# One tiling for value and background matmuls: 128-wide matmuls written as four column tiles

## The chip, the cores and the metric

The kernel runs on one core of one Trainium2 chip. The metric is the device time of one execution in microseconds; the median of three runs stands for a kernel. Durations and waits come from one profiled execution. In its rows PE is the matmul engine (TensorE), PEld its weight loads, DVE, ACT and POOL are the vector, activation and general engines, SP issues DMAs.

## The reference

A transformer block over 2048 rows of 640 values in bfloat16: layer norm, attention with 32 heads of 20, a residual, a second layer norm, a gated feed-forward of 1728 with a second residual.

```python
def _A_ref(x, wqkv, wo):
    ...
    scores = jnp.einsum("bhqd,bhkd->bhqk", q, k) * (Dh ** -0.5)
    p = _softmax(scores, axis=-1)
    o = jnp.einsum("bhqk,bhkd->bhqd", p, v)
    ...
h = x + _A_ref(_layernorm(x, axis=-1), A_wqkv, A_wo)
# _B_ref: h_ = gelu(x @ w_gate) * (x @ w_up); return h_ @ w_down
h2 = h + _B_ref(_layernorm(h, axis=-1), B_w_gate, B_w_up, B_w_down)
```

## The kernel before

**Chunks and slots.** The rows are cut into seven query chunks of 512, 512, 256, 256, 256, 128 and 128 rows, numbered 0 to 6. The heads form eight groups of four; a slot is one group at 512 rows, two at 256, four at 128. A slot goes through all 2048 keys in units of two or three score tiles of 512 columns, held in the PSUM banks 0 to 2 and 3 to 4 in turn.

**Three kinds of matmul.** A score matmul (line 919, helper `qk_mms`) has 32 rows of weights, the tile position (32 j, 0) for head j of the group, and so a row tile of the array. A value matmul (`pv_op`, recorded at line 359 with `v_all` among its inputs) uses all 128 rows and 21 columns of weights, 20 values and a column of ones for the sum, at the tile position (0, 32 j): four heads sit beside each other as four column tiles and write four strips of 32 partitions of bank 6. All others use the whole 128 x 128 array: projections of q, k, v and of the attention output (`chain`, line 640; wo is the latter's weight), gate and up (`mms`, line 1095), down (line 1159), transposes (lines 585 and 1002), bounds of the scores (`q_bound`, line 732, 32 columns of weights, and `q_bound0`, line 752), and warming matmuls that write nothing of use.

**Around them.** ACT takes exponentials of the score tiles; a part of the tiles goes to DVE instead (line 840 and the operations after it), which approximates the exponential by sums of four terms. After a slot, DVE copies bank 6 to `osb`, the sums go through small DMAs and a reciprocal, POOL scales, and DMAs put the rows into memory. `post` then does for one chunk: loading the attention rows, wo, residual (line 1063), layer norm, transposition (by DMA, for the last chunk on PE), gate, gelu (by tanh on ACT, or by its table for the last chunk), up and product (lines 1131, 1148, 1120), down, residual (line 1163) and the output DMA. It runs while the next chunk's scores are being made; these "background" operations use the banks that are left, 7 and 5.

**Who sets the order.** The program is listed as operations with their engine, estimated duration, priority, inputs and outputs. `Sched.schedule` plays them through a model of the engines and writes one fixed order per engine; `emit` adds the semaphores. Priorities go from scores (0) over value matmuls (1), slot ends (2) and layer norm (2.5) to background (3). Every PE operation has a mode, "row", "col" or "full". A change of mode costs 0.098 us in the model. Lines that use it:

```python
MODE_SWITCH = {"pe": .098, "act": 1.28}
...
if chosen is None:
    chosen, banks = o, got
    if e != "pe" or p[0] < 1 or o.mode == mode[e] or t - o.ready > PE_AGE:
        break
elif o.mode == mode[e]:
    chosen, banks = o, got
    break
```

So PE takes the ready operation of highest priority, but below the scores it prefers one of the present mode, unless the first has been ready for over 1.5 us (PE_AGE). An operation below the scores is not started if it, with its switch, would run past the time at which the next scores are due. Where PE would be idle for long, the model inserts warming matmuls.

## Time and profile before

| what | value |
|---|---|
| median of 3 runs | 899.54 us (898.82 to 899.83) |
| profiled execution: its own time, its span | 899.9 us, 898.2 us |
| PE busy | 836.4 us |
| ACT busy | 851.0 us |
| DVE busy | 689.6 us |
| matmuls of PE, weight loads | 10745, 10809 |
| mean granted clock of PE | 0.998 |

The span is the time from the first to the last instruction of the profiled execution; the rest of its own time lies around it. A busy PE is not a PE at its peak: matmuls are pipelined, a busy stretch includes their latency and short pauses between them. The start of one matmul less the start of the one before says more than the duration of either. A row such as "128\*21 128x256" names the weights (128 rows, 21 columns) and the streamed operand (128 partitions, 256 columns). Some matmul records are missing, so that the weight loads of a line count its matmuls better.

### The profile page before, as it was taken

How to read it: one execution, taken by the hardware profiler on the slowest of the kernel's cores; microseconds unless marked ns; L12 is line 12 of the kernel's file. 1: busy time of each engine (PE TensorE's matmuls, PEld its weight loads, DVE VectorE, ACT ScalarE, POOL GpSimd, SP SyncE). 2: the span in 40 equal slices, each digit the busy share in tenths (PEclk: the TensorE clock that was granted, in tenths of full speed). 3: DMA queues.
4: the chain of work that ended last, by engine and by line, in shares of the span. 5: the costliest groups of instructions: out<-in, count | busy, mean ns of one | idle time of the engine just before them, and what ended most of it. 6: DMA issues, size and time to landing. Idle time of an engine off the chain costs nothing.

```text
span 898.2 us, 24425 instructions
## 1 busy us (share of the span) xinstructions
PE 836.4 (93%) x10745; PEld 359.1 (40%) x10809; DVE 689.6 (77%) x1263; ACT 851.0 (95%) x777; POOL 75.0 (8%) x147
## 2 busy tenths in 40 slices
PE   3999999899989899999999899999999999999988
PEld 2532222222223222323344333334445446666657
DVE  7839888888989888787778889965669669658553
ACT  6699999999999999999999999999999999999960
POOL 5000000000001100000000100000102000020100
PEclk9999999999999999999999999999999999999999
DMA  7211120222244510000111110011111010031000
GB/s 264 84 50 49 32 67 29 64 81 66 73 137 135 152 46 17 17 14 5 39 51 54 33 34 17 18 30 48 29 54 33 18 48 18 20 63 26 10 17 15
DMA packets 55937, 46.17 MB, mean 51 GB/s; under 512 B 25492, under 2 KB 49392, under 8 KB 55832
## 3 DMA queue, kind: packets, MB, share of 16 engines
q1 hardware_dynamic: 55832, 44.62, 17.8%
q8 instruction: 84, 1.38, 0.6%
q14 instruction: 21, 0.17, 0.1%
HBM read 30.68 MB, written 11.04 MB: 46 GB/s over the span
## 4 chain that ended last, share of the span: by engine, by line
ACT 46%; PE 46%; DVE 6%; issue 1%; DMA 1%; DVEq 0%
ACT pts L359 35%; PE ps L919 14%; PE ps L359 11%; ACT rege L359 10%; PE ps L1095 9%; PE ps L640 6%; PE ps L1159 5%; DVE rege L359 1%; DVE qt_all L359 1%; DVE rege L840 1%; ACT qt_all L359 1%; DVE stats L359 1%; DVE rege L1131 1%; PE ps L585 1%; DMA rege<-xn_t 1%
## 5 line engine op out<-in xcount | busy, mean ns | idle before, releaser
L359 ACT ACTIVATE pts<-ps 128x1536 bf16<-128x1536 f32 x578 | 652.6, 1242 | 10.2 <-PE ps L919 5.7
L919 PE MATMUL ps<-qt_all,kt_all 32*128 32x256 bf16 (+2 forms) x3584 | 320.8, 288 | 25.7 <-ACT pts L359 16.7
L919 PEld LDWEIGHTS ps<-qt_all,kt_all 32*128 32x128 bf16 x3584 | 103.3, 92 | 236.0 <-ACT pts L359 128.3
L840 DVE TENSOR_SCALAR rege<-ps 128x512 int16<-128x512 f32 x200 | 137.0, 687 | 58.6 <-PE ps L919 56.4
L359 ACT ACTIVATE rege<-ps 128x1536 bf16<-128x1536 f32 x115 | 172.1, 1496 | 1.5 <-PE ps L359 0.7
L1095 PE MATMUL ps<-rege,regw 128*128 128x256 bf16 (+2 forms) x951 | 151.6, 289 | 8.4 <-DVE rege L359 2.9
L359 PE MATMUL ps<-pts,v_all 128*21 128x256 bf16 (+2 forms) x2472 | 134.0, 287 | 0.0
L359 PE MATMUL ps<-rege,v_all 128*21 128x512 bf16 (+2 forms) x1564 | 127.6, 312 | 1.3 <-DVE rege L359 1.0
L840 DVE TENSOR_SCALAR qt_all<-ps 128x512 int16<-128x512 f32 x116 | 79.8, 688 | 42.5 <-PE ps L919 40.9
L1095 PEld LDWEIGHTS ps<-rege,regw 128*128 128x128 bf16 x980 | 74.2, 99 | 65.7 <-issue 31.5
L359 POOL TENSOR_TENSOR on<-osb,bsum 128x512 bf16<-128x512 f32 x30 | 42.0, 1399 | 648.2 <-DMA bsum<-rsums 648.1
L359 DVE TENSOR_SCALAR rege<-rege 128x2048 int16<-128x2048 int16 x132 | 92.7, 717 | 2.1 <-PE ps L359 1.2
L640 PE MATMUL ps<-regw 128*128 128x512 bf16 (+1 forms) x340 | 82.0, 349 | 4.6 <-issue 1.7
L1159 PE MATMUL ps<-regw,rege 128*128 128x320 bf16 x448 | 83.7, 302 | 1.1 <-DVE rege L1120 0.5
L359 PEld LDWEIGHTS ps<-pts,v_all 128*21 128x21 bf16 x2472 | 54.3, 91 | 32.4 <-issue 24.4
L359 DVE TENSOR_SCALAR qt_all<-qt_all 128x2048 int16<-128x2048 int16 (+2 forms) x111 | 64.7, 594 | 2.0 <-PE ps L359 1.0
L359 PEld LDWEIGHTS ps<-rege,v_all 128*21 128x21 bf16 x1564 | 41.0, 90 | 45.9 <-issue 23.6
L359 PE MATMUL ps<-qt_all,v_all 128*21 128x256 bf16 (+2 forms) x1048 | 53.7, 282 | 1.7 <-DVE qt_all L359 1.6
L1159 PEld LDWEIGHTS ps<-regw,rege 128*128 128x128 bf16 x448 | 36.6, 97 | 35.8 <-issue 20.1
L359 DVE TENSOR_SCALAR qt_all<-rege 128x2048 int16<-128x2048 int16 x70 | 48.9, 707 | 0.9 <-PE ps L359 0.4
L640 PEld LDWEIGHTS ps<-regw 128*128 128x128 bf16 x360 | 28.9, 98 | 47.5 <-issue 25.0
L1148 DVE TENSOR_TENSOR rege<-rege,ps 128x512 bf16<-128x512 bf16 (+1 forms) x53 | 35.8, 677 | 15.6 <-PE ps L1095 15.4
(98 smaller groups left out, 503.2 us busy)
## 6 DMA issues: line engine op xcount, KB each, us to landing
bsum<-rsums SPq DMA_DIRECT2D x120, 64.0 KB, 2.0
rege<-in_A_x_dram SPq DMA_DIRECT2D x6, 640.0 KB, 5.1
q_rows<-regw SPq DMA_DIRECT2D x20, 128.0 KB, 1.9
out_dram<-rege SPq DMA_DIRECT2D x16, 160.0 KB, 2.2
attn<-on SPq DMA_DIRECT2D x120, 20.0 KB
regw<-in_B_w_gate_dram SPq DMA_DIRECT2D x5, 432.0 KB, 3.3
regw<-in_B_w_up_dram SPq DMA_DIRECT2D x5, 432.0 KB, 3.2
kt_all<-k_rows SPq DMA_DIRECT2D x12, 160.0 KB
```

Of the source, the lines that this page charges most:

```text
L359: return lambda eng: getattr(eng, method)(*args, **kwargs)
L585: op("pe", lambda eng, a=a: eng.transpose(bank16(bk, D)[:, 128 * a:128 * a + 128], src[:, a * 128:(a + 1) * 128], ident[:]), 0.055, prio, ...
L640: yield op("pe", lambda eng, l=l, r=r, k=k: eng.matmul(bank(bk, n), l, r, start=(k == 0), stop=(k == len(steps) - 1)), c_mm(n), prio, mode ...
L840: d_ops.append(op("dve", lambda eng: eng.tensor_scalar(v[:, 512 * h:512 * h + 512], bank(b), EXP_MUL, -32000.0, ALU.mult, ALU.max), c_dve( ...
L919: return lambda eng: eng.matmul(out()[:, kk * nq:(kk + 1) * nq], kt_all[32 * j:32 * j + 32, g, kt * 128:(kt + 1) * 128], qt_all[32 * j:32 ...
L1095: op("pe", lambda eng, a=a, f=f, fi=fi: eng.matmul(bank(bk)[:, fi * nq:(fi + 1) * nq], w[:, a, F0[f]:F0[f] + 128], hnT[:, a, 128 * tb:128 ...
L1131: op("dve", lambda eng, bg=bg, fv=fv, w=w: eng.tensor_scalar(fv, bank(bg, w), 0.5, None, ALU.mult), c_dve(w), p, reads=[kg], writes=hkeys( ...
L1148: hdone.append(op("dve", lambda eng, bu=bu, fv=fv, w=w: eng.tensor_tensor(fv, fv, bank(bu, w), ALU.mult), c_dve(w), p, reads=[ku] + hkeys( ...
L1159: op("pe", lambda eng, f=f, o=o, hf=hf, bk=bk: eng.matmul(bank(bk, 320), ha_f[:, o:o + 128], wd[:, f, hf * 320:(hf + 1) * 320], start=(f = ...
```

## The change

A new helper `col4` writes a matmul with 128 columns of weights as four with 32 columns each, at the tile positions (0, 0), (0, 32), (0, 64) and (0, 96), each into its strip of 32 partitions of the same bank, all with the same streamed operand. The four are one operation with the estimated duration of one. It is used in `chain` (all projections and wo), `mms` (gate and up), down and the warming matmuls. The matmuls of `q_bound` keep their number and get the tile position (0, 0). All these now have the mode "col", as value matmuls have. Transposes and `q_bound0` stay "full".

```diff
-                                o.fns, o.mode = [self.warm[b]], "full"
+                                o.fns, o.mode = self.warm[b], "col"
...
-                yield op("pe", lambda eng, l=l, r=r, k=k: eng.matmul(
-                    bank(bk, n), l, r, start=(k == 0), stop=(k == len(steps) - 1)),
-                    c_mm(n), prio, mode="full", util=n / 2400.0, reads=reads, writes=[key], acq=[bk] if (k == 0 and acq) else [],
+                yield op("pe", col4(lambda bk=bk: bank(bk, n), l, r, k == 0, k == len(steps) - 1),
+                    c_mm(n), prio, mode="col", util=n / 2400.0, reads=reads, writes=[key], acq=[bk] if (k == 0 and acq) else [],
                     after=after if k == 0 else ())
+
+        def col4(out, l, r, start, stop):
+            return [lambda eng, j=j: eng.matmul(out()[32 * j:32 * j + 32], l[:, 32 * j:32 * j + 32], r, start=start, stop=stop,
+                                                tile_position=(0, 32 * j), skip_group_check=True) for j in range(4)]
...
-                    bank(bk)[0:32, :], sel[:, t, :], aq[t], start=(k == 0), stop=(k == len(ts) - 1)),
-                    c_mm(512), prio, mode="full", util=0.05, reads=[aqk(t), ("sel", t)], writes=[key],
+                    bank(bk)[0:32, :], sel[:, t, :], aq[t], start=(k == 0), stop=(k == len(ts) - 1),
+                    tile_position=(0, 0), skip_group_check=True),
+                    c_mm(512), prio, mode="col", util=0.05, reads=[aqk(t), ("sel", t)], writes=[key],
...
-                        op("pe", lambda eng, a=a, f=f, fi=fi: eng.matmul(
-                            bank(bk)[:, fi * nq:(fi + 1) * nq], w[:, a, F0[f]:F0[f] + 128], hnT[:, a, 128 * tb:128 * tb + nq],
-                            start=(a == 0), stop=(a == NA - 1)),
-                           c_mm(nq), p, mode="full", util=nq / 2400.0, reads=hk + [(wkey, 0)], writes=[key], acq=[bk] if st else [],
+                        op("pe", col4(lambda fi=fi: bank(bk)[:, fi * nq:(fi + 1) * nq], w[:, a, F0[f]:F0[f] + 128],
+                                      hnT[:, a, 128 * tb:128 * tb + nq], a == 0, a == NA - 1),
+                           c_mm(nq), p, mode="col", util=nq / 2400.0, reads=hk + [(wkey, 0)], writes=[key], acq=[bk] if st else [],
...
-                        op("pe", lambda eng, f=f, o=o, hf=hf, bk=bk: eng.matmul(
-                            bank(bk, 320), ha_f[:, o:o + 128], wd[:, f, hf * 320:(hf + 1) * 320],
-                            start=(f == 0), stop=(f == NF - 1)), c_mm(320), p, mode="full", util=0.133, reads=hkeys(f // fn_) + [("wd", 0), "wd2", "wdz"],
+                        op("pe", col4(lambda bk=bk: bank(bk, 320), ha_f[:, o:o + 128], wd[:, f, hf * 320:(hf + 1) * 320],
+                                      f == 0, f == NF - 1), c_mm(320), p, mode="col", util=0.133, reads=hkeys(f // fn_) + [("wd", 0), "wd2", "wdz"],
...
-        sc.warm = {b: I("matmul", PS[:, 512 * b:512 * b + 512], kt_all[:, 0, 0:128], kt_all[:, 0, 0:512], start=True, stop=True,
-                        skip_group_check=True) for b in sc.warm_banks}
+        sc.warm = {b: col4(lambda b=b: PS[:, 512 * b:512 * b + 512], kt_all[:, 0, 0:128], kt_all[:, 0, 0:512], True, True)
+                   for b in sc.warm_banks}
```

## The prediction

> **What bounds the kernel now.** I read the page first: shares of engines, then the chain.

> ```profile
> span 898.2 us, 24425 instructions
> ...
> PE 836.4 (93%) x10745; PEld 359.1 (40%) x10809; DVE 689.6 (77%) x1263; ACT 851.0 (95%) x777; POOL 75.0 (8%) x147
> ...
> ACT 46%; PE 46%; DVE 6%; issue 1%; DMA 1%; DVEq 0%
> ```

> ACT and PE are both near full and share the chain, so neither share says where a saving counts. The busy time by stretches does:

> ```profile
> 725.00:750.00 25.00, 25.00 (x394) 13.63 (x393) 18.21 (x32) 24.85 (x23) 1.28 (x1) 1.00 0.13 37
> 775.00:800.00 25.00, 25.00 (x654) 15.74 (x640) 16.84 (x34) 24.73 (x23) 4.57 (x15) 1.00 0.23 41
> 850.00:875.00 25.00, 20.55 (x377) 14.88 (x377) 12.47 (x33) 17.01 (x19) 0.00 (x0) 0.96 0.05 15
> 875.00:900.00 25.00, 19.84 (x260) 17.28 (x257) 7.49 (x14) 2.96 (x6) 0.00 (x0) 0.97 0.04 14
> ```

> Columns after the length: PE, PEld, DVE, ACT, POOL, granted clock, DMA. From 50 to 859 us ACT runs exponentials back to back (their last ends at 858.9, from ACT's timeline); there a faster PE cannot move ACT by more than the few waits it has. From 859 on ACT is nearly idle, and 39.3 us are left. PE's timeline shows what fills them:

> ```profile
> 858.22 2.35 PE L1159 MATMUL ps<-regw,rege 128*128 128x320 bf16 x16
> 860.41 0.33 PE L1095 MATMUL ps<-rege,regw 128*128 128x128 bf16 x3
> ...
> 873.54 0.93 PE L1095 MATMUL ps<-rege,regw 128*128 128x128 bf16 x7 [2.87 <-DVE rege L359]
> ...
> 874.80 6.57 PE L1095 MATMUL ps<-rege,regw 128*128 128x128 bf16 x101
> 881.20 3.97 PE L1159 MATMUL ps<-regw,rege 128*128 128x320 bf16 x28
> 885.01 5.86 PE L1095 MATMUL ps<-rege,regw 128*128 128x128 bf16 x102
> 891.38 3.98 PE L1159 MATMUL ps<-regw,rege 128*128 128x320 bf16 x28 [0.52 <-DVE rege L1120]
> ```

> A chunk of 128 rows has 70 gate, 70 up (L1095) and 28 down (L1159) matmuls. So the last 16 down matmuls of chunk 4 and the whole feed-forward of chunk 5 come after the last exponential, although chunk 5's attention ended at 801.5 (copy of its accumulator): background work is late. Of 101 + 102 after 874.80, 140 are chunk 6's own, 63 chunk 5's.

> **What the change removes.** Switches of PE's tiling. One stretch of PE's timeline has them all:

> ```profile
> 846.78 0.42 PE L919 MATMUL ps<-qt_all,kt_all 32*128 32x128 bf16 x12
> 847.13 0.63 PE L359 MATMUL ps<-pts,v_all 128*21 128x128 bf16 x32
> 847.69 0.45 PE L1159 MATMUL ps<-regw,rege 128*128 128x320 bf16 x2
> 848.07 0.40 PE L919 MATMUL ps<-qt_all,kt_all 32*128 32x128 bf16 x12
> ```

> Score matmuls (row tiles) start at 846.78, value matmuls (column tiles) at 847.13, full ones at 847.69, scores at 848.07. Eight steps of four value matmuls at 56 ns are 0.45 us, yet the next group starts 0.56 later: 0.11 for the switch. Two of 320 columns (0.136 each) take 0.27 of 0.38: 0.11 again. Over the timeline of PE, start of a group less start and streaming time of the last matmul before, the median is 91 to 101 ns for each of the six kinds. There are 1627 switches, about 160 us of PE; 223 are between column and full tiles and cost nothing afterwards: 223 x 0.098 = 21.9 us. Those from and to row tiles stay, as every score group stands between two others. By time: 60 before 270 us, 140 from 270 to 747, 22 to 859, 1 later. Before 270 there is no feed-forward to be late (chunk 0's starts at 308), so I count 162 x 0.098 = 15.9 us.

> **What it adds.** About 2019 full matmuls (counted by their weight loads: 980 L1095, 448 L1159, 520 L640, 71 warming) become 8076, with as many weight loads of 32 columns. The nearest row is the value matmul: four of them start 3 to 4 ns apart, and the next four follow after 56 ns (128 columns) or 109 (256); full steps have 56 and 109, and 216 at 512 in both inside a run. The four tiles stream beside each other, with new weights at every step. Hence zero per step is my value. The bounds: the first step of a value run is 7 to 8 ns longer (117 at 256), and each new step is an operation of its own with its own semaphore update, so +8 a step is possible; weight loads of 32 columns (L732, not tiled) take 93 against 90 to 91 of the value's 21, and four in series would add 12 more: 0 to 20 ns a step; nothing below, since streaming is no shorter. Issue: the densest 128 PE instructions of the trace take 1.0 us, the densest 256 take 2.8; the tail's steps of 128 columns need 256 in 1.8. If the queue were held to 2.8, a step would take 88 ns and the 203 late ones 6.5 us more; I take 0, as the 128 go at the needed rate, and keep 6.5 as the end.

> Transposes (L585, L1002) stay full, so their neighbours now switch: 11 times from 17 to 28 us, 6 in the tail. At the start at most 11 x 0.1 = 1.1 us, in part under PE's waits for ACT and DVE: 0.5. In the tail two of three groups lie on the path: 0.4. Score bounds (L732) change tiling only, at the same length. The written order is planned anew, with value and background matmuls in one class: no switch is charged between them, so background fits into more gaps, and value matmuls go first instead of waiting behind a run of full ones. ACT's excess over its steady pitch between 50 and 868 us is some 20 us in all, near 1 us per 50 outside the ends; I move it by nothing and keep 2 us each way.

> **Sum.** From 803 to 860 PE gets through chunk 4's feed-forward (140 x 0.109 + 56 x 0.136 = 22.9 us) and chunk 5's wo (1.4): 43% of the time. Its start at 802.9 waited for the transposed rows (DMA, 0.25), not for PE; but their wo began at 775.65, when the attention rows (issued 763.90, 3.4 us to landing) had been there for 8 us, while PE was full (25.00 of 25). The 13.7 us saved from 270 to 747 clear that queue, so I take those 8 us and no more: the data cap it. Saved from 747 to 859: 2.2 us, or 5 us of elapsed time at 43%. Chunk 4 then ends at 860.4 - 13 = 847.4, just after chunk 5's rows are there (transpose issued 842.2, 2.7 us). Until 858.9 PE does 11.5 x 0.43 = 4.9 us of chunk 5's 12 (140 x 0.056 + 28 x 0.136 = 11.6, and gaps). The 7.1 left fit between 859 and 874.8, where chunk 6's own path (transposes, wo, switches) needs 3.4 of 15.9 us and PE waits 4.5 us today. So 63 x 0.062 + 28 x 0.137 = 7.8 us go from the end. What is late next is chunk 6's own chain, wo, layer norm, gate, up, down. Back come 0.5, 0.4 and 0.2 for a longer half-clock stretch (13 steps of 107 ns at 875 now, after an idle PE). 898.2 - 7.8 + 1.1 = 891.5 of span; the profiled execution took 899.9, 1.7 more, so 893.2; it lies 0.4 above the median 899.54: **892.8 us**. If chunk 5's tanh no longer delays the square root (table load at 871.2, after tanh at 870.1), the norm comes 1 to 2 us sooner: own range 888 to 896.

> [...] The trace has value steps with four weight loads of 21 columns every 56 ns. [...]

> **Rivals.**
> 1. Forecast: backlog cleared, 0.55.
> 2. Weight loads bind the short steps, 0.08. If the value's 56 ns already were the limit of its 84 columns, 128 columns take 85: +29 on 140 steps of chunk 6 and some 60 others, 4 to 6 us, which eats most of the gain: 897 to 899, and up to 902 if twice that. Against it: 21 and 32 columns differ by 3 ns as rows. [...]
> 3. Nothing is gained, 0.12: chunk 4 and 5 are held by banks and DMA chains, not PE (start at 802.9 after a DMA), so the tail stays: 898 to 901.
> 4. Slower, 0.25: each four-tile step costs p more than the planner is told, on all 1600 background steps after 270. It gains 15.9 and loses 1600 p; from p = 10 ns the backlog grows, and all of it lands in the tail. At 15 ns: +8.1, 907.6; at 20: +16, 915.6. PE at 25.00 of 25 gives it no room; interior value steps at 56 and 109 speak against it.

> That the switches stay is excluded by the value groups: tiles of one tiling follow each other at 56 ns.

> Faster by over 0.2% (1.8 us, about what a measurement of this kernel can tell from no change): 0.55. Within: rival 3 and half of 2, 0.16. Slower: rival 4 and half of 2, 0.29. The range for 8 in 10: 887.5, below the forecast's own, to 908, which leaves out rival 4 beyond 15 ns.

> **What would show it.** Right: no 0.1 us between value and background groups; chunk 4's last down before 850; fewer than 70 L1095 of chunk 5 after 859; the last L1095 group after 874 with some 140 steps, not 203; last exponential at 859 within 2 us. Wrong: four-tile steps over 66 ns at 128 or 119 at 256 (rivals 2, 4); ACT waiting for L919 between 50 and 859; a tail of 39 us as now (rival 3).

## The result and the profile after

The changed kernel takes **921.43 us** (median of 4 runs, 920.31 to 926.06), the kernel before 899.68 beside it: ratio 1.0253, 95% interval 1.0221 to 1.0284. It is slower by 21.8 us, outside the predicted range. The profiled execution is the longest of its four (926.06), so its sums are some 4 us larger than the difference of the medians. A helper takes the lines on by about four: scores are L923 now, every four-tile matmul has the line of `col4`, L645.

The page of the changed kernel, the same lines as before:

```profile
span 924.3 us, 36732 instructions
...
PE 851.3 (92%) x16930; PEld 375.0 (41%) x16930; DVE 687.7 (74%) x1263; ACT 853.1 (92%) x777; POOL 73.3 (8%) x147
...
ACT 46%; PE 39%; DVE 8%; DMA 4%; issue 2%; POOL 1%; SPq 0%; DVEq 0%; POOLq 0%
```

PE's matmuls and weight loads have grown from 21,554 to 33,860, by what the prediction counted and 16 more warming operations (87, before 71). The busy times of ACT and DVE are within 2.1 us of those before, so for them the 26.1 us of span are idle time. I cut the span at the first and at the last exponential of the scores (ACT's timeline):

| | before | changed | difference |
|---|---|---|---|
| first exponential starts | 35.6 | 38.6 | +3.0 |
| first to last exponential | 823.3 | 839.4 | +16.1 |
| last exponential to the end ("tail") | 39.2 | 46.3 | +7.1 |

**The middle.** The 693 exponentials come in the same order in both kernels, so the delay of each against the kernel before can be read. It is 2.9 us at the first and 0.3 from the ninth on (48 us): the late start is made up. At the last it is 19.0.

ACT's waits for scores have grown (total, times, longest; before, the first row was 5.7, 7, 3.7):

```profile
ACT pts L359 <- PE ps L923: 20.7, 25, 5.3
ACT rege L359 <- PE ps L923: 5.2, 7, 1.5
```

Busy time by stretches says where. Here ACT (fourth engine) is below 22 of 25 us, and so is the granted clock (three columns from the end), which was 1.00 in all stretches of the kernel before up to 850:

```profile
75.00:100.00 25.00, 23.55 (x250) 6.53 (x249) 18.64 (x35) 21.04 (x20) 1.27 (x1) 0.80 0.12 32
125.00:150.00 25.00, 23.52 (x238) 6.12 (x240) 18.45 (x35) 20.79 (x19) 1.27 (x1) 0.73 0.21 53
275.00:300.00 25.00, 22.27 (x218) 5.61 (x216) 14.42 (x26) 16.57 (x14) 1.27 (x1) 0.66 0.49 152
```

The clock was at half for 10.2 us from 84.3, 13.7 from 135.5 and 17.1 from 282.3, 41.0 us in all. From the start of each of these stretches to 3 us behind its end the delay grows from 0.1 to 3.5, from 3.9 to 8.8 and from 9.5 to 17.9 us: 16.7 of the 19.0 us arise there. PE's timeline just ahead of the first of them:

```profile
79.98 0.39 PE L923 MATMUL ps<-qt_all,kt_all 32*128 32x512 bf16 x3
80.31 0.39 PE L735 MATMUL ps<-sq,sel 128*32 128x512 bf16 x1
81.33 1.61 PE L923 MATMUL ps<-qt_all,kt_all 32*128 32x512 bf16 x8 [0.63 <-ACT pts L359]
83.34 0.32 PE L645 MATMUL ps<-regw 128*32 128x320 bf16 x4 [0.41 <-DVE rege L844]
```

For three microseconds PE has little but scores, which wait for ACT to free their banks; no value or background group stands between them. PE looks busy, as a score matmul of 512 columns is recorded for 0.39 us, but little streams through it. Count each matmul by its columns / 2400 us, as the kernel's own `util` does (0.213 us for 512 columns, where the traces have 0.216 from step to step), and by a quarter of that if it is one of four tiles, row or column. Then PE streams some 0.2 of its time in the 3.4 us from 80.2; in the kernel before no 3.4 us between 50 and 860 us fall much below 0.3 (the lowest has 0.28, at 115.9).

**The tail.** PE's timeline at its end:

```profile
902.03 3.28 PE L645 MATMUL ps<-rege,regw 128*32 128x128 bf16 x203
907.09 1.97 PE L645 MATMUL ps<-rege,regw 128*32 128x128 bf16 x128 [1.78 <-issue]
911.11 1.97 PE L645 MATMUL ps<-rege,regw 128*32 128x128 bf16 x128 [2.05 <-issue]
914.86 1.61 PE L645 MATMUL ps<-rege,regw 128*32 128x128 bf16 x101 [1.77 <-issue]
917.07 4.41 PE L645 MATMUL ps<-regw,rege 128*32 128x320 bf16 x112 [0.60 <-DVE rege L1123]
```

128 matmuls with 128 weight loads are 256 instructions. They run at the full rate (32 steps in 1.8 us, 56 ns each) and then PE stands for 1.8 to 2.1 us with nothing to wait for that the profile shows ("issue"). The DMA rows name the limit: the queue of kind "instruction" that serves PE has 132 packets of 16 KB here (84 before), one for each 256 of its 33,860 recorded instructions (21,554 before), and never two within 3.3 us (smallest distance 3.35). From the last exponential on these pauses add up to 10.3 us.

### The profile page after: what moved, and what is told of

Same layout as the page of the kernel before. It is cut to its first block, busy times and chain, and to the rows that moved or that the text cites. A ratio compares the mean times of both kernels' runs of the same rounds, so it can differ in the third digit from the quotient of the medians.

```text
span 924.3 us, 36732 instructions
## 1 busy us (share of the span) xinstructions
PE 851.3 (92%) x16930; PEld 375.0 (41%) x16930; DVE 687.7 (74%) x1263; ACT 853.1 (92%) x777; POOL 73.3 (8%) x147
## 4 chain that ended last, share of the span: by engine, by line
ACT 46%; PE 39%; DVE 8%; DMA 4%; issue 2%; POOL 1%; SPq 0%; DVEq 0%; POOLq 0%
ACT pts L359 35%; PE ps L645 18%; PE ps L923 12%; ACT rege L359 9%; PE ps L359 9%; DVE rege L844 2%; DMA regw<-in_A_wqkv_dram 1%; DVE qt_all L359 1%; DVE qt_all L844 1%; ACT qt_all L359 1%; DMA rege<-xn_t 1%; DMA sums<-osb 1%; DVE rege L359 1%; PE ps L585 0%; DVE xn_t L359 0%
## 5 line engine op out<-in xcount | busy, mean ns | idle before, releaser
L359 ACT ACTIVATE pts<-ps 128x1536 bf16<-128x1536 f32 x578 | 656.0, 1258 | 22.0 <-PE ps L923 20.7
L923 PE MATMUL ps<-qt_all,kt_all 32*128 32x256 bf16 (+2 forms) x3584 | 324.1, 292 | 21.9 <-ACT pts L359 14.4
L923 PEld LDWEIGHTS ps<-qt_all,kt_all 32*128 32x128 bf16 x3584 | 101.2, 92 | 260.5 <-ACT pts L359 145.3
L645 PE MATMUL ps<-rege,regw 128*32 128x256 bf16 (+2 forms) x3920 | 166.0, 289 | 16.4 <-issue 10.3
L359 ACT ACTIVATE rege<-ps 128x1536 bf16<-128x1536 f32 x115 | 173.6, 1510 | 5.6 <-PE ps L923 5.2
L359 PE MATMUL ps<-pts,v_all 128*21 128x256 bf16 (+2 forms) x2472 | 136.7, 291 | 0.0
L359 PE MATMUL ps<-rege,v_all 128*21 128x512 bf16 (+2 forms) x1564 | 132.3, 321 | 1.5 <-DVE rege L359 1.2
L844 DVE TENSOR_SCALAR qt_all<-ps 128x512 int16<-128x512 f32 x116 | 79.7, 687 | 41.3 <-PE ps L923 39.6
L645 PEld LDWEIGHTS ps<-rege,regw 128*32 128x32 bf16 x3920 | 81.9, 96 | 61.7 <-issue 32.5
L645 PE MATMUL ps<-regw 128*32 128x512 bf16 (+1 forms) x1440 | 94.5, 360 | 4.7 <-DVE rege L844 2.4
L359 DVE TENSOR_SCALAR rege<-rege 128x2048 int16<-128x2048 int16 x132 | 88.8, 690 | 4.0 <-PE ps L359 3.4
L359 POOL TENSOR_TENSOR on<-osb,bsum 128x512 bf16<-128x512 f32 x30 | 38.8, 1293 | 639.0 <-DMA bsum<-rsums 639.0
L645 PE MATMUL ps<-regw,rege 128*32 128x320 bf16 x1792 | 82.3, 301 | 2.3 <-DVE rege L1151 1.2
L359 PEld LDWEIGHTS ps<-pts,v_all 128*21 128x21 bf16 x2472 | 53.1, 91 | 36.0 <-issue 30.8
L359 DVE TENSOR_SCALAR qt_all<-qt_all 128x2048 int16<-128x2048 int16 (+3 forms) x111 | 63.2, 583 | 1.9 <-PE ps L359 0.9
L359 PEld LDWEIGHTS ps<-rege,v_all 128*21 128x21 bf16 x1564 | 42.1, 91 | 41.2 <-issue 21.1
L359 PE MATMUL ps<-qt_all,v_all 128*21 128x256 bf16 (+2 forms) x1048 | 55.2, 284 | 1.6 <-DVE qt_all L359 1.1
L645 PEld LDWEIGHTS ps<-regw 128*32 128x32 bf16 x1440 | 34.8, 98 | 45.7 <-issue 19.1
L645 PEld LDWEIGHTS ps<-regw,rege 128*32 128x32 bf16 x1792 | 42.1, 96 | 25.0 <-issue 10.6
L359 DVE TENSOR_SCALAR qt_all<-rege 128x2048 int16<-128x2048 int16 x70 | 48.9, 709 | 0.9 <-PE ps L359 0.4
```

The source lines that it names most:

```text
L359: return lambda eng: getattr(eng, method)(*args, **kwargs)
L645: return [lambda eng, j=j: eng.matmul(out()[32 * j:32 * j + 32], l[:, 32 * j:32 * j + 32], r, start=start, stop=stop, tile_position=(0, 32 ...
L844: d_ops.append(op("dve", lambda eng: eng.tensor_scalar(v[:, 512 * h:512 * h + 512], bank(b), EXP_MUL, -32000.0, ALU.mult, ALU.max), c_dve( ...
L923: return lambda eng: eng.matmul(out()[:, kk * nq:(kk + 1) * nq], kt_all[32 * j:32 * j + 32, g, kt * 128:(kt + 1) * 128], qt_all[32 * j:32 ...
```

## The experiments

Theory A: the middle is lost by lulls in the new order, in which PE's granted clock falls to half; the tail by the fetch of PE's instructions; the start by the order. Theory B: four-tile matmuls count less than full ones for what halves the clock. Each expectation was on record before its run.

**Old order, new instructions.** Every `mode="col"` of the change is "full" again for the planner; what is written stays four tiles.

```diff
-                    c_mm(n), prio, mode="col", util=n / 2400.0, ...
+                    c_mm(n), prio, mode="full", util=n / 2400.0, ...
```

> Four-tile instructions as in the changed kernel, but the planner is told the old modes, so every engine has the order of the kernel before. Theory A (the half-clock stretches at 84, 135 and 282 us come from lulls in the new order; the tail from PE's instruction fetch): no half clock before 860, first exponential at 35.6 and last at 859 within 2 us, but the tail has pauses of 1 to 2 us after every 256 PE instructions and is 46 to 51 us long instead of 39: 906 to 912. Theory B (column tiles count less for the clock gate than full matmuls do): half-clock stretches between 75 and 300 us here too, last exponential 868 or later, 915 or more.

Measured: 907.71 us, 1.0086 (1.0058 to 1.0115). First exponential 36.7, last 856.2, no half clock before 870, tail 48.2 with pauses of 0.5 to 1.9 us. The same stretches of this kernel:

```profile
75.00:100.00 25.00, 23.06 (x309) 7.34 (x309) 21.03 (x37) 24.46 (x22) 1.27 (x1) 1.00 0.11 31
125.00:150.00 25.00, 23.18 (x312) 7.53 (x308) 20.57 (x36) 24.95 (x23) 1.27 (x1) 1.00 0.06 18
275.00:300.00 25.00, 22.73 (x316) 7.02 (x308) 23.48 (x49) 25.00 (x24) 6.02 (x15) 1.00 0.43 126
```

The clock is full and ACT too, with the four-tile instructions of the changed kernel. Theory B falls.

**New order, old instructions.** `col4` writes one full matmul.

> The order of the changed kernel, but with full 128 x 128 matmuls again, so that switches between value and background groups, which this order does not plan for, cost some 0.1 us each on PE. Theory A: half-clock stretches near 84, 135 and 282 us as in the changed kernel, first exponential 38.6, last 875 or later; no pauses at 256 instructions in the tail, which is 39 us or less: 908 to 925. Theory B: no half clock before 860, last exponential 861 to 868, 900 to 908.

Measured: 933.99 us (runs from 922.56 to 937.08, the longest of them profiled), 1.0333 (1.0262 to 1.0405). First exponential 38.7; half clock for 51.2 us, from 75.3, 246.0 and 293.7; last exponential 900.6; tail 34.7 without pauses. The order alone brings the late start and the half clock. The size was missed. Of the 41.7 us by which its last exponential is late, 19.9 arise in the half-clock stretches. Another 13.5 come after 315 us, at full clock; that fits the 327 switches between value and background groups that this order does not plan, about 0.1 us each in this trace, but was not tested by itself.

**Parts of the change.** First with the projections, bounds and warming matmuls full, then with the chunks of 128 rows full as well.

```diff
+        def one(out, l, r, start, stop):
+            return [lambda eng: eng.matmul(out(), l, r, start=start, stop=stop, skip_group_check=True)]
...
-                        op("pe", col4(lambda fi=fi: ...
+                        op("pe", (col4 if nq > 128 else one)(lambda fi=fi: ...
```

> Projections of q, k and v, bounds and warming matmuls full as before, in mode and instruction; wo, gate, up and down in four tiles. Theory A: first exponential at 35.6, and no half clock near 84 and 135 us, since the old order of chunk 0 is back; the one near 282 may stay (8 us) or go; the tail has the pauses and is 45 to 47 us: 903 to 913. Theory B: no half clock before 250 either (few four-tile matmuls there), but one after 300 us where feed-forward is all there is: 912 or more.

Measured: 913.17 us, 1.0144 (1.0117 to 1.0171). First exponential 36.2, one half-clock stretch of 3.4 us at 130, last 864.1, tail 48.1. The time lies 0.2 us above theory A's range and within theory B's, the tail 1 us above A's, and A had no half clock near 135 us; but what B asks for, half clock after 300 us, is not there.

> As the one with full projections, and besides it the chunks of 128 rows keep full matmuls for wo, gate, up and down. If the pauses in the tail are PE's instruction fetch, they go, the tail is 39 us or less and the time lies 6 to 10 us below that of the kernel with full projections alone: 893 to 901. If the pauses have another cause (short steps of any kind), the tail stays at 45 us or more and the time within 2 us of that kernel.

Measured: 903.25 us, 1.0047 (1.003 to 1.0064), 9.9 below the run before it; tail 39.1 without pauses. The tail is settled, but the time was expected at 893 to 901: the backlog should have shrunk, and did not.

**The fetch by itself.** The kernel before, with only gate and up of the chunks of 128 rows written in m tiles of 128 / m columns, planned as before. With m = 4 a step of 56 ns has 8 PE instructions, with m = 2 it has 4, so that 256 of them last 3.6 us.

```diff
+                        op("pe", [lambda eng, a=a, f=f, fi=fi, j=j: eng.matmul(
+                            bank(bk)[64 * j:64 * j + 64, fi * nq:(fi + 1) * nq], w[:, a, F0[f] + 64 * j:F0[f] + 64 * j + 64],
...
+                            tile_position=(0, 64 * j), skip_group_check=True) for j in range(2)] if nq == 128 else
```

> The kernel before, with only gate and up of the chunks of 128 rows as four tiles of 32 columns, planned as before: 8 PE instructions a step. Fetch theory: pauses of 1.2 to 2.2 us after each 256 instructions in the tail, which grows by 7 to 9 us to 46 to 48; exponentials end at 859 as before: 906 to 909.

Measured: 908.62 us, 1.0096 (1.0063 to 1.0129); last exponential 857.9, tail 47.2.

> The kernel before, with gate and up of the chunks of 128 rows as two tiles of 64 columns: 4 PE instructions a step instead of 2, and planned as before. If the limit is one fetch of 256 instructions per 3.4 to 3.7 us, 64 steps of 56 ns (3.6 us) just fit: pauses of 0.2 us or less at each block, tail 39 to 40.5 us, time 899 to 901. [...]

Measured: 901.1 us, 1.0014 (0.9999 to 1.0029); tail 39.0. PE's timeline, four tiles first:

```profile
887.66 3.75 PE L1095 MATMUL ps<-rege,regw 128*32 128x128 bf16 x255
893.32 1.97 PE L1095 MATMUL ps<-rege,regw 128*32 128x128 bf16 x127 [1.91 <-issue]
897.23 0.57 PE L1095 MATMUL ps<-rege,regw 128*32 128x128 bf16 x26 [1.94 <-issue]
```

and two tiles, the same 102 steps:

```profile
883.84 5.88 PE L1095 MATMUL ps<-rege,regw 128*64 128x128 bf16 x204
```

With two tiles there is not one pause, and the steps are those of full matmuls (102 in 5.86 us before). It is the count of instructions, not tiling as such: twice the instructions cost nothing, four times cost 8.2 us of tail (47.2 against 39.0; 39.2 in the kernel before).

**The half clock by itself.** Two runs: the changed kernel with more warming, and the kernel before with none.

```diff
-WARM_WIN, WARM_MIN = 3.4, 0.5
+WARM_WIN, WARM_MIN = 3.4, 0.65
```

> The changed kernel, with the planner's bound for warming raised from 0.5 to 0.65 of PE's time in 3.4 us, so that it fills lulls with more warming matmuls. Theory A (lulls in the new order bring the half clock, which holds up ACT by some 16 us): the half-clock stretches before 300 us go, exponentials end at 860 to 866, the tail keeps its pauses: 904 to 911. If the half clock is no consequence of lulls, it stays and the time is 918 or more.

Measured: 921.19 us, 1.0247 (1.0214 to 1.0279). The half clock went from 41.0 to 6.8 us before the last exponential and the middle from 839.4 to 829.9, as A has it; but the last exponential was at 869.4, not 860 to 866, and the tail grew to 51.0, so the time did not move. The middle's part is confirmed, the forecast of the time was a miss: with some 90 more warming operations the rest of the order changed as well. The last exponential is 10.4 us late, of which the two half-clock stretches left take 1.6; what takes the rest stays open. Of the 4.7 us that the tail is longer than in the changed kernel, some 2.5 are 19 down steps of chunk 4 after the last exponential, where the changed kernel has none, and 1.3 a half-clock stretch at 912.2 in the last down group (5.66 us instead of 4.41).

> The kernel before without its warming matmuls (bound 0 instead of 0.5), nothing in tiles. It measures the price of a half clock without four-tile matmuls: in the changed kernel 41 us of it went with 16 us that ACT lost, 0.4 us each. Theory A: half-clock stretches appear in lulls between 100 and 530 us, and ACT loses 0.3 to 0.5 us for each us of them, so with 20 to 50 us of half clock the time is 906 to 922. If the half clock does not cost ACT's time, the time stays within 3 us of 900 with half-clock stretches in the trace.

Measured: 922.7 us, 1.0247 (1.0215 to 1.028). Without one four-tile matmul there are 64.9 us of half clock in eight stretches before the last exponential, which comes at 878.7, 19.8 late; 18.8 of that arise in these stretches. The tail is 39.6. ACT's excess over its steady pitch (the middle less 798.9 us) rises from 24.4 to 44.1: 0.30 us for each us of half clock (0.39 in the changed kernel: 40.5 - 24.4 over 41.0, or 0.41 by the 16.7 us above). The time is 0.7 us above the expected range. One of its stretches:

```profile
75.00:100.00 25.00, 24.45 (x167) 6.04 (x166) 17.02 (x28) 18.84 (x17) 1.26 (x1) 0.67 0.08 20
```

PE is busy for 24.45 of 25 us there at a mean granted clock of 0.67, more than in the kernel before at 1.00 (23.17; at half clock a step of 128 columns lasts longer too, 107 ns instead of 56 in the kernel before from 873 to 876.4): a high busy share in the profile does not say that the clock will hold.

**What is left of the gain.** Three mixtures, with the projections and the chunks of 128 rows full. In the first two the planner knows the real modes, and chunks 0 to 3, or 0 and 1, have four tiles in wo, gate, up and down.

> Projections full, four tiles only in wo, gate, up and down of chunks 0 to 3; chunk 4 (256 rows, whose feed-forward runs beside value steps of 128 columns) and the chunks of 128 rows full. If the fetch of PE instructions held chunk 4's feed-forward back between 800 and 860 us (one fetch per 3.4 to 4 us there), it now ends 4 us or more before the last exponential, the tail is 34 to 37 us, and the time 896 to 899. If data and banks held it, chunk 4's last down stays 2 us or more behind the last exponential and the time is 900 to 903.

Measured: 903.17 us, 1.003 (1.0017 to 1.0043). Last exponential 860.3, tail 41.1. Chunk 3's feed-forward ends at 787.1 instead of 802.7, 15.6 us earlier, and then PE's timeline has this (L649 with `kt_all` alone is warming):

```profile
800.60 0.60 PE L649 MATMUL ps<-kt_all 128*128 128x512 bf16 x2
801.14 0.63 PE L925 MATMUL ps<-qt_all,kt_all 32*128 32x128 bf16 x24
801.70 0.60 PE L649 MATMUL ps<-kt_all 128*128 128x512 bf16 x2
802.60 0.39 PE L649 MATMUL ps<-kt_all 128*128 128x512 bf16 x1 [0.29 <-DVE rege L846]
```

The planner warms, because there is no work: chunk 4's attention rows were issued at 770.2 (763.9 before), its wo residuals ran from 782.9 to 793.7 (776.5 to 785.3), its transposes were issued at 803.1 and 804.4 (796.8 and 798.1). Its last residual is at 864.4 (860.6 before). The time saved on PE is there and is spent waiting for chunk 4's data. These are later from their source on: the accumulator of chunk 4's last slot was copied at 750.4 (746.0 before).

> The same with four tiles only in the chunks of 512 rows (0 and 1), where a step takes 216 ns and the fetch has most room. Switches saved after 660 us come back, so the backlog is as before: 899 to 902 by either theory; a gain of over 2 us would say that only the early switches matter, a loss of over 2 us that the new order itself costs, whatever the tiles do.

Measured: 901.33 us, 1.0018 (1.0003 to 1.0033): first exponential 36.4, last 861.6, tail 37.9. As expected, no gain.

Last, the old order with four tiles only in chunks 0 to 3.

> Order of the kernel before (old modes for the planner); four tiles only in wo, gate, up and down of chunks 0 to 3, all else full. It holds what the experiments leave of the gain: no new lulls, no added switches at the start, no fetch limit. Theory A: first exponential at 35 to 36, no half clock before 860, ACT's excess over its pitch 1 to 3 us less than before (24.4), tail 39: 897 to 899, at the edge of what can be told from no change. If the removed switches are worth nothing where ACT is full, the excess is as before and the time within 1 us of it; 902 or more would say that four tiles cost something even here.

Measured: 900.47 us against 900.41, 0.9999 (0.9987 to 1.0011); first exponential 36.3, excess 24.7 against 24.4, tail 39.3. That is the second branch, but not for its reason. At 53 us the exponentials are 0.7 us later than in the kernel before, at 759 they are 1.8 us earlier, so the shorter PE was worth 2.5 us; at 778 they are 0.9 later. Between 759 and 778 chunk 3 has its feed-forward, and PE's timeline has four pauses, with exactly 256 instructions from each to the next, in the middle of groups of scores (L925), gate or up (L645) and values (L359):

```profile
759.41 0.32 PE L925 MATMUL ps<-qt_all,kt_all 32*128 32x128 bf16 x3 [0.47 <-issue]
763.43 0.83 PE L645 MATMUL ps<-rege,regw 128*32 128x256 bf16 x23 [0.47 <-issue]
767.72 0.40 PE L925 MATMUL ps<-qt_all,kt_all 32*128 32x128 bf16 x11 [0.63 <-issue]
771.46 0.29 PE L359 MATMUL ps<-pts,v_all 128*21 128x128 bf16 x7 [0.86 <-issue]
```

These 2.4 us of fetch take the gain back before the tail begins. The first run with the old order, with one pause of 0.2 us there, shows the gain too: its exponentials are 0.8 us late at 53 us, 2.8 early at 760 and 2.7 early at the end. Without four tiles ahead of the chunks of 128 rows (the two runs on the fetch by itself) they drift by 0.1 and 0.3 us from 53 to 760. So where ACT is full a shorter PE is worth a little, as long as its instructions come. The same with four tiles in the projections and in chunk 4 too, but not in the chunks of 128 rows:

> Order of the kernel before (old modes for the planner), four-tile instructions everywhere but in wo, gate, up and down of the chunks of 128 rows. Theory A: exponentials end at 856 as in the first run with the old order (their wait for scores is shorter, as value and background groups follow each other without a switch), the tail is 39 us again: span 895 to 896, time 896.5 to 898, faster than before by 0.2 to 0.3%. If the short four-tile steps are not what prolongs the tail, 905 or more.

Measured: 901.17 us, 1.0016 (1.0004 to 1.0028), a miss by 3 to 5 us: first exponential 37.5, 3.4 us of half clock at 129.9, last at 859.7, tail 39.6. The first run with the old order had a middle of 819.5 us, 2.7 shorter than this one with nearly the same instructions. Their traces show where: this one falls back by 1.4 us at its half-clock stretch and by 1.1 at each of two pauses, 0.82 us at 771.3 and 0.67 at 826.4, where the first run has 0.2 and 0.3. Why the same place is starved in one and not in the other stays open. No version beat the kernel before; one with four tiles only ahead of 750 us in the old order was not run.

## Why the prediction was wrong

**Right: switches and steps.** The medians between value and background groups fell from 99 and 101 ns to -6 and 1, and those from and to scores stayed at 91 to 99. Four-tile steps have 56, 109 and 216 ns at 128, 256 and 512 columns, and 136 at 320 (medians): zero per step held between fetches, with no sign of slower weight loads (95 to 99 ns is the mean of those of 32 columns, 97 to 99 that of the same lines' loads of 128 columns before). The rivals that put a price on each step (2 and 4) did not happen; rival 4 named the right sign by the wrong mechanism. Of the other signs of being right one came: the last gate-and-up group has 140 steps, not 203 (the 560 matmuls from 902.03 on). Chunk 4's last down came at the last exponential (878), not before 850, and all 140 gate and up steps of chunk 5 came after it, not fewer than 70.

**The step that failed first: "I move it by nothing and keep 2 us each way".** ACT's time from its first to its last exponential grew by 16.1 us, and the last one came 19.0 us later. I had read that value matmuls would go first and background fit into more gaps, and costed it at nothing, because ACT was full. I did not ask what PE would be doing after the work had been packed together. With one mode for both, work is done sooner, and stretches follow in which PE has scores only; there the clock halves, and at half clock PE no longer keeps up with ACT (16.7 us). Order alone does it (second run), the instructions alone do not (first run), and taking the warming from the kernel before does the same (19.8 us). In the other direction "nothing" was wrong as well: in the old order the removed switches bring the exponentials forward by 2.5 to 3.6 us between 53 and 760 us.

**Issue: "I take 0 ... and keep 6.5 as the end".** Measured 8.2 us by itself, and 10.3 us of pauses in the changed kernel, which has four tiles in wo and down as well. The range came from the densest 256 instructions of the trace (2.8 us), but part of those had been fetched ahead: they start at 767.9, and the instruction DMAs from 764.0 to 773.2 lie 4.8 and 4.3 us apart. The rate that holds for a long stretch is the distance of the instruction DMAs, of which the trace of before had the smallest at 3.46 us; 256 instructions in 3.5 us are 110 ns for a step of eight, and 203 late steps at 110 instead of 56 are 11 us.

**"So I take those 8 us".** Chunk 4's feed-forward did not start earlier. With the queue ahead of it cleared by 15.6 us (four tiles in chunks 0 to 3), its first gate matmul is at 808.5 instead of 802.9, as the data chain from the end of its attention was later: rival 3, held by banks and DMA chains. In the changed kernel wo followed its rows after 2.5 us instead of 8.4, but the rows were issued 23.7 us after the accumulator's copy instead of 17.9. So chunk 4 does not end 13 us earlier in any version. Part of the 7.8 us at the end came all the same: the new order with full matmuls (second run) has a tail of 34.7, 4.5 less than before, and in the changed kernel the pauses hide it. With the chunks of 128 rows full at most 1.3 us of it is there (tails of 37.9 to 41.1).

**The start: 0.5.** The first exponential was 3.0 later, but 2.6 of that were made up by the ninth, so the term itself was not too small. Not the 11 switches cost the 3.0, but the planner's avoidance of them: with transposes "full" and projections "col" it does 40 of the transposes in one go (22.95 to 25.9 us) before the projections that the first scores need. Projections in four tiles in the old order put the first exponential at 36.7 and 37.5; in the new one, full or not, it is at 38.6 to 39.5.

## What to carry to other kernels

Removing a cost from an engine in a kernel with a planned order is a change of the order: ask what the planner does with the time, and whether the data for it are there. A time that did not move can be a gain and a loss of the same size: compare the start of the same instruction in both traces along the way. Before multiplying PE's instructions, divide the distance of its instruction DMAs by 256 (here 3.35 us at the least, 13 ns) and compare it with the time that an instruction has in the longest dense stretch (56 ns for eight in the four-tile tail, 7 ns each). Look at the granted clock by stretches first: it was 0.67 in 25 us of which PE was busy for 24.45.

## What the runs showed of the hardware

The half-clock stretches that end within these traces last whole multiples of 3.41 us (3.41 to 27.31; 10.24, 13.65 and 17.07 in the changed kernel), and within one execution they begin whole multiples of it apart (84.3, 135.5 and 282.3: 15 and 43). In the windows of this grid, over all runs with half clock and by the count of columns above, the 18 windows just ahead of a halving streamed 0.20 to 0.40 of their time, 11 of them under 0.32; of some 2600 others at full clock between 45 and 870 us none was under 0.32. Between 0.33 and 0.40 the count does not decide: in the changed kernel 0.38 at 132.1 was followed by half clock, 0.39 at 521.2 was not.
